# The second gate's row made on chip, and the last four chunks' second weights multiplied by it on GpSimd

## The chip, the cores and the metric

The kernel runs on one core of a Trainium2 chip. The metric is device time in microseconds (us) of one execution; the lower the better. Engines are named as in the profile: PE is TensorE (matmuls; PEld is its weight load), DVE is VectorE, ACT is ScalarE, POOL is GpSimd, and SP is the queue that issues most DMAs.

## The reference

One transformer block on 2048 tokens of width 640 (32 heads of 20), with six modulation rows from a condition vector `c`, and a squared-relu feed-forward layer of width 1728:

```python
mod = (_silu(c) @ w_mod).reshape(c.shape[0], 6, 1, -1)
sa, ca, ga, sb, cb, gb = (mod[:, 0], mod[:, 1], mod[:, 2], mod[:, 3], mod[:, 4], mod[:, 5])
h = _layernorm(x, axis=-1) * (1 + ca) + sa
x = x + ga * _A_ref(h, A_wqkv, A_w_phi, A_wo)
h = _layernorm(x, axis=-1) * (1 + cb) + sb
x = x + gb * _B_ref(h, B_w1, B_b1, B_w2, B_b2)
```

`_A_ref` is linear attention whose feature map is a pair of softmaxes over each head's 20 numbers (`exp` of q and of -q after a small matrix per head); `_B_ref` is `relu(h @ w1 + b1)**2 @ w2 + b2`. The change concerns `gb`, the row of 640 numbers that multiplies the feed-forward result.

## The kernel before

Every fp32 product is made of three fp32r matmuls: each operand is split into a high part (ACT copies it, `AF.Copy`) and a low part (DVE subtracts the high part from the whole, `lo`, line 88), and the terms are high by high, high by low, low by high (`three`, line 78 issues all of them). So each operand of PE costs ACT one copy and DVE one subtraction ahead of it, and the third matmul of a group is the first to need the low part.

Work goes in three stages. First q, k and v are projected for 16 token tiles of 128, and k's and v's sums over tokens are collected. Then, from about 255 us to 389 us, attention's second half runs over eight pairs of tiles, `j` from 0 to 7 in the loop around line 1135: DVE scales the feature rows (`e_prod`, `e_recip`, `e_scale`), PE turns them (`tr_e`, tiles te, whose PSUM banks come from a pool of three), ACT copies them out (tiles ept), PE multiplies by k's and v's sums (`num`), ACT and DVE split that (`num_hi`, `num_lo`, tiles ot), and PE multiplies by the output weights (`do_wo`, tiles pwo). The pair's PE work is interleaved by hand: pair j's four `do_wo` pieces with pair j+1's `tr_e` and `num`. Four q tiles had been put off, and their feature maps are made inside this loop: `q_chain(KEPT + ..., False)` is DVE's part (two reductions, two subtractions, tiles mxq and eq), `exps` is ACT's.

The third stage is the feed-forward layer, eight blocks of 256 tokens (`j` from 0 to 7 again), 14 chunks of 128 hidden columns each (the last has 64), two chunks to a pair `n`. `up` makes a chunk (15 matmuls), ACT applies the relu (line 1250), DVE squares it (line 1251), ACT and DVE split it (`split_a`, tiles ra), and the products with w2 follow one pair later (`down`), between the two `up`s of the next pair. From block 2 on most pairs use seven products in place of eight: DVE makes four sums of quarter tiles (line 1265), ACT and DVE split these (`split_s`, tiles rs), and some combinations of w2's quarters come from DRAM through rings of four SBUF buffers, whose DMAs POOL issues (`t_fetch`, line 1360) when PE has finished with a buffer. The last block takes pairs 4 to 6 plainly. Its accumulators lie in PSUM banks acc (regions 1, 2, 4, 5), acc3x (regions 3 and x share one) and acc67.

The order on PE, DVE, ACT and POOL is written by hand in both later stages (in the third, SP's too, but for block 1); each engine works its queue in order. The gate's row `gb_b` (128 equal rows of 640) multiplies the result of each block (`by_gate`), and `bb` is b2 times that row, added to the residual (`add_bias`, `XR`). In the before kernel the gate lies as a column per 128 numbers (`gate_b`, 128x5); `spread_row` writes it to DRAM number by number and reads it back as a row to all partitions. In the last block the gate multiplies the sum of pairs 0 to 3 (`first_combos`, then `by_gate` at line 1418), and the four quarters of the rest one by one at the very end (`last_downs`): product into the same accumulators, `by_gate` into a spare tile `end`, `add`, `store`.

## Time and profile before

| what | value |
| --- | --- |
| median of 3 runs | 769.13 us (768.96 to 769.65) |
| the profiled execution, its own time | 769.86 us |
| span of its instructions | 768.2 us |
| granted TensorE clock over the span | 1.0 |
| busy share: PE, DVE, ACT, POOL | 99%, 77%, 57%, 19% |

The profiled execution's time is 1.66 us above its span (what lies around the first and last instruction) and 0.73 us above the median. A row of the timeline is: start in us, duration in us, engine, line, operation, output<-inputs, shapes, count; in brackets stands how long the engine sat idle before it and what released it. Consecutive like instructions are merged into one row. A row of the groups ends with busy us and the mean ns of one instruction.

### The profile page before, as it was taken

The page shows a single profiled execution, that of the slowest core. Times are in us where ns is not written, and L with a number is a line of the kernel's source. Part 1 is how long each engine was busy: PE and PEld are TensorE (multiplying, and loading weights), DVE is VectorE, ACT ScalarE, POOL GpSimd, SP SyncE. Part 2 cuts the span into 40 slices and gives each one's busy share as a digit, 9 for nine tenths or more (in the row PEclk, how much of TensorE's full clock was granted, in tenths as well). Part 3 has the DMA queues.
Part 4 walks back from the last instruction along what each step waited for, and adds up shares of the span by engine and source line. Part 5 has one row for each costly group of instructions (what it writes and reads, how often), then busy time and mean ns, then how long its engine had stood idle before and what let it go on. Part 6 is the DMA issues. An engine that isn't in the chain of part 4 may idle for free.

```text
span 768.2 us, 15300 instructions
## 1 busy us (share of the span) xinstructions
PE 759.3 (99%) x5967; PEld 739.8 (96%) x5967; DVE 593.8 (77%) x1083; ACT 434.6 (57%) x971; POOL 144.2 (19%) x301
## 2 busy tenths in 40 slices
PE   9999999999999999999999999999999999999997
PEld 8999999999999989888999999999999999999996
DVE  6598897989999999999565667866767666675666
ACT  5766756767843454545776647465553636445331
POOL 3001101101100255442101000231321313222110
PEclk9999999999999999999999999999999999999999
DMA  9811431343333344155356367996766758766450
GB/s 327 305 65 73 137 103 54 104 139 114 119 104 109 117 142 170 70 80 160 107 180 222 110 226 253 286 323 195 226 181 197 232 177 262 221 184 192 130 165 35
DMA packets 52151, 126.69 MB, mean 165 GB/s; under 512 B 7335, under 2 KB 8103, under 8 KB 52079
## 3 DMA queue, kind: packets, MB, share of 16 engines
q1 hardware_dynamic: 34744, 84.65, 33.1%
q0 software_dynamic: 14752, 35.76, 16.7%
q10 hardware_dynamic: 2583, 5.30, 1.8%
q8 instruction: 47, 0.77, 0.4%
q14 instruction: 25, 0.20, 0.1%
HBM read 95.70 MB, written 29.89 MB: 163 GB/s over the span
## 4 chain that ended last, share of the span: by engine, by line
PE 85%; DVE 8%; issue 2%; DMA 2%; POOL 2%; ACT 1%; SPq 0%; POOLq 0%; DVEq 0%
PE up L78 23%; PE acc L78 17%; PE pk L78 9%; PE pv L78 9%; PE pq L78 8%; PE pwo L78 5%; PE acc3x L78 5%; PE kvp L450 3%; DVE dn L879 2%; DVE scr L877 2%; DVE ezb L901 1%; PE tb L357 1%; PE te L921 1%; DMA ring_b<-td_b 1%; PE ta L357 1%
## 5 line engine op out<-in xcount | busy, mean ns | idle before, releaser
L78 PE MATMUL up<-h,w 128*128 128x256 f32 x1640 | 206.4, 278 | 0.0
L78 PEld LDWEIGHTS up<-h,w 128*128 128x128 f32 x1640 | 196.1, 188 | 0.0
L1250 ACT ACTIVATE ft<-up,b_t 128x256 f32<-128x256 f32 x104 | 48.9, 470 | 115.1 <-PE up L78 114.6
L78 PE MATMUL acc<-w,ra 128*128 128x384 f32 x452 | 97.4, 335 | 0.0
L1251 DVE TENSOR_TENSOR ft<-ft 128x256 f32<-128x256 f32 x104 | 44.1, 424 | 51.2 <-ACT ft L1250 49.6
L78 PE MATMUL pwo<-wo,ot 128*128 128x256 f32 (+3 forms) x512 | 80.8, 312 | 0.6 <-DVE ot L88 0.6
L78 PEld LDWEIGHTS pwo<-wo,ot 128*128 128x128 f32 (+1 forms) x512 | 74.5, 188 | 3.8 <-issue 2.7
L78 PE MATMUL pq<-wq,hT 128*128 128x384 f32 (+1 forms) x480 | 75.2, 312 | 0.0
L78 PEld LDWEIGHTS acc<-w,ra 128*128 128x128 f32 x452 | 72.7, 188 | 0.7 <-DVE ra L88 0.5
L78 PE MATMUL pk<-wk,hT 128*128 128x384 f32 (+1 forms) x480 | 72.7, 308 | 0.0
L78 PE MATMUL pv<-wv,hT 128*128 128x384 f32 (+1 forms) x480 | 71.7, 307 | 0.0
L78 PEld LDWEIGHTS pq<-wq,hT 128*128 128x128 f32 x480 | 71.1, 188 | 0.6 <-issue 0.2
L78 PEld LDWEIGHTS pk<-wk,hT 128*128 128x128 f32 x480 | 70.5, 188 | 0.4 <-issue 0.2
L78 PEld LDWEIGHTS pv<-wv,hT 128*128 128x128 f32 x480 | 70.1, 188 | 0.0
L88 DVE TENSOR_TENSOR ra<-ft,ra 128x384 fp32r<-128x384 f32 (+2 forms) x86 | 36.8, 448 | 32.9 <-ACT ra L1274 20.2
L78 PE MATMUL acc3x<-w,ra 128*128 128x256 f32 x248 | 42.3, 278 | 1.4 <-DVE end L1418 1.4
L1360 POOL DMA_DIRECT2D ring_a<-td_a x34 | 18.3, 537 | 125.5 <-PE acc L78 103.2
L1274 ACT ACTIVATE ra<-ft 128x384 fp32r<-128x384 f32 x48 | 25.2, 526 | 28.4 <-DVE ft L1251 22.4
L78 PEld LDWEIGHTS acc3x<-w,ra 128*128 128x128 f32 x248 | 39.5, 188 | 1.8 <-DVE end L1418 1.6
L1265 DVE TENSOR_TENSOR ft<-ft 128x128 f32<-128x128 f32 x136 | 33.3, 286 | 1.2
L441 DVE TENSOR_REDUCE sk<-ek 128x64 f32<-128x1280 f32 x16 | 23.7, 1484 | 12.4 <-ACT ek L436 10.8
L885 POOL TENSOR_TENSOR dn<-dn,rs_q 128x32 f32<-128x32 f32 x32 | 20.1, 629 | 68.1 <-DVE dn L879 67.8
(264 smaller groups left out, 1406.5 us busy)
## 6 DMA issues: line engine op xcount, KB each, us to landing
ring_c<-td_c POOLq DMA_DIRECT2D x34, 384.0 KB, 4.0
ring_a<-td_a POOLq DMA_DIRECT2D x34, 384.0 KB, 4.1
ring_b<-td_b POOLq DMA_DIRECT2D x34, 256.0 KB, 4.0
esp<-eq SPq DMA_DIRECT2D x12, 640.0 KB, 3.2
el<-esp SPq DMA_DIRECT2D x12, 640.0 KB, 4.0
rw<-in_w SPq DMA_DIRECT2D x23, 320.0 KB, 3.1
wm<-in_w_mod SPq DMA_DIRECT2D x20, 320.0 KB, 3.7
xb<-in_x SPq DMA_DIRECT2D x8, 640.0 KB, 4.0
```

The source lines that it names most:

```text
L78: nc.tensor.matmul(o, a, b, start=first and i == 0, stop=last and i == len(terms) - 1, skip_group_check=skip,)
L88: (eng or nc.vector).tensor_tensor(out_lo, full, hi.bitcast(F32), op=ALU.subtract)
L357: nc.tensor.transpose(p[:, i * P : (i + 1) * P], xn[:, i, d * P : (d + 1) * P], ident)
L441: nc.vector.tensor_reduce(s, heads(flat(e)), axis=AX.X, op=ALU.add)
L450: nc.tensor.matmul(kvp[g // 4][64 * c : 64 * c + 64, a : a + 2 * n].rearrange("p (s n) -> p s n", s=2), v[:, u], e[:, :, o : o + n], start ...
L877: nc.vector.tensor_tensor(z, flat(ET[t]), flat(zb), op=ALU.mult)
L885: nc.gpsimd.tensor_tensor(dn[:, s], dn[:, s], rs[:, 1 - s], op=ALU.mult)
L1250: nc.scalar.activation(r, p, AF.Relu, bias=b1_t[:, f : f + 1])
L1251: nc.vector.tensor_tensor(r, r, r, op=ALU.mult)
L1265: nc.vector.tensor_tensor(t[:, o], t[:, a], t[:, b], op=op)
L1274: nc.scalar.activation(a[:, 0, :3], t[:, :3], AF.Copy)
L1360: nc.gpsimd.dma_start(RING[j, n, r], TD[n][r].bitcast(F32R))
```

## The change

It has three parts.

1. **The gate's row.** `mod_sum(5, gate_b)`, a DVE reduction, moves from the end of pair j = 3 to j = 6. The column is turned by one small PE transpose at j = 7 into 5 rows of 128, copied by ACT (`gate_r`), written to DRAM as whole rows and read back by the same broadcast. b2 is loaded into `bb` itself, early; the product `bb * gb_b` moves from j = 5 to block 0, pair 4.
2. **Attention's orders.** For j = 1 to 5 the second batch of `tr_e` goes (3, 4, 5) in place of (5, 3, 4). At j = 1 DVE's part of the put-off feature map, `q_chain`, stands ahead of `num_lo` in place of behind it.
3. **The end.** The second weights of chunks 10 to 13 are loaded once more in the last block (SP), multiplied by the gate's row on POOL (`gated_mul`, in pairs 1 to 4), and split by ACT and DVE (`gated_split`). So the products of pairs 5 and 6 need no gate: they go to fresh accumulators (`last2`, `last4`, `last3`, `lastx`), in the order 2, 4, 3, x, and at the end one DVE `add` for each follows. The old accumulators are closed after pair 4 and taken through the gate while `up` of pair 6 runs (`piece`). The two bias adds of the last block's residual move from DVE to POOL.

DVE's queue in attention's pair j = 1, before (ezb: scaled features; ot: low parts of the numerator that PE multiplies by the output weights; mxq, eq: the put-off feature map; scr: the next tile's product):

```order
L906 TENSOR_TENSOR ezb_3165<-el_3429,dn_3597 128x80
L88 TENSOR_TENSOR ot_3726<-numa_3727,ot_3726 128x2x256
L88 TENSOR_TENSOR ot_3726<-numb_3728,ot_3726 128x2x256
L88 TENSOR_TENSOR ot_3726<-numc_3729,ot_3726 128x256
L88 TENSOR_TENSOR ot_2_3742<-numc_3729,ot_2_3742 40x256
L430 TENSOR_REDUCE mxq_3769<-eq_2839 128x32
L431 TENSOR_REDUCE mxq_3769<-eq_2839 128x32
L433 TENSOR_TENSOR eq_2839<-eq_2839,mxq_3769 128x640 x2
L877 TENSOR_TENSOR scr_3167<-el_3611,zb 128x1280
```

and the same place after:

```order
L905 TENSOR_TENSOR ezb_3165<-el_3429,dn_3597 128x80
L430 TENSOR_REDUCE mxq_3706<-eq_2840 128x32
L431 TENSOR_REDUCE mxq_3706<-eq_2840 128x32
L433 TENSOR_TENSOR eq_2840<-eq_2840,mxq_3706 128x640 x2
L88 TENSOR_TENSOR ot_3731<-numa_3732,ot_3731 128x2x256
L88 TENSOR_TENSOR ot_3731<-numb_3733,ot_3731 128x2x256
L88 TENSOR_TENSOR ot_3731<-numc_3734,ot_3731 128x256
L88 TENSOR_TENSOR ot_2_3747<-numc_3734,ot_2_3747 40x256
L876 TENSOR_TENSOR scr_3167<-el_3611,zb 128x1280
```

The four instructions of the feature map passed the four that make ot; nothing else moved there.

POOL's queue in the last block's pairs 1 and 2, before (ring: the ring buffers that POOL's DMAs fill; the first number is the pair):

```order
L1360 DMA ring_1_a<-td_a 128x768
L1360 DMA ring_1_b<-td_b 128x512
L1360 DMA ring_2_c<-td_c 128x768
L1360 DMA ring_2_a<-td_a 128x768
L1360 DMA ring_2_b<-td_b 128x512
```

and after, on to the end (w2g: w2's rows as loaded, multiplied in place; xr: the residual):

```order
L1368 TENSOR_TENSOR w2g_8969<-w2g_8969,gb_b 128x640
L1380 DMA ring_1_b<-td_b 128x512
L1380 DMA ring_2_c<-td_c 128x768
L1380 DMA ring_2_a<-td_a 128x768
L1368 TENSOR_TENSOR w2g_9045<-w2g_9045,gb_b 128x640
L1380 DMA ring_2_b<-td_b 128x512
L1380 DMA ring_3_c<-td_c 128x768
L1380 DMA ring_3_a<-td_a 128x768
L1368 TENSOR_TENSOR w2g_9128<-w2g_9128,gb_b 128x640
L1380 DMA ring_3_b<-td_b 128x512
L1368 TENSOR_TENSOR w2g_9207<-w2g_9207,gb_b 128x640
L1667 TENSOR_TENSOR xr_7_0_9210<-xr_7_0_9210,bb 128x640
```

A multiply now stands between the ring DMAs a and b of each pair; the last multiply and the two adds (the second is the queue's last) stand in a row.

DVE's last instructions, before (ft: the chunk; ra: its parts; end: the scratch for the gate; y: the result):

```order
L88 TENSOR_TENSOR ra_6_9396<-ft_6_9393,ra_6_9396 128x128 x2
L1255 TENSOR_TENSOR ft_6_9393<-up_9401,ft_6_9393 64x256
L1256 SCALAR_TENSOR_TENSOR ft_6_9393<-ft_6_9393 64x256
L88 TENSOR_TENSOR ra_6_9396<-ft_6_9393,ra_6_9396 64x256
L1415 TENSOR_TENSOR y_0_9302<-y_0_9302,xr_7_0_9192 128x640
L1415 TENSOR_TENSOR y_1_9303<-y_1_9303,xr_7_1_9194 128x640
L1418 TENSOR_TENSOR end<-acc3x_9076,gb_b 128x256
L1415 TENSOR_TENSOR y_0_9302<-y_0_9302,end 128x256
L1418 TENSOR_TENSOR end<-acc3x_9076,gb_b 128x256
L1415 TENSOR_TENSOR y_1_9303<-y_1_9303,end 128x256
L1418 TENSOR_TENSOR end<-acc_7_9025,gb_b 128x384
L1415 TENSOR_TENSOR y_0_9302<-y_0_9302,end 128x384
```

(region 4's two follow) and after (xr is now the scratch for the gated pieces; last, lastx: the fresh accumulators):

```order
L88 TENSOR_TENSOR ra_6_9422<-ft_6_9419,ra_6_9422 128x128 x2
L1444 TENSOR_TENSOR xr_7_0_9210<-acc_7_9032,gb_b 128x384
L1441 TENSOR_TENSOR y_0_9322<-y_0_9322,xr_7_0_9210 128x384
L1260 TENSOR_TENSOR ft_6_9419<-up_9429,ft_6_9419 64x256
L1261 SCALAR_TENSOR_TENSOR ft_6_9419<-ft_6_9419 64x256
L88 TENSOR_TENSOR ra_6_9422<-ft_6_9419,ra_6_9422 64x256
L1444 TENSOR_TENSOR xr_7_1_9212<-acc_7_9036,gb_b 128x384
L1441 TENSOR_TENSOR y_1_9323<-y_1_9323,xr_7_1_9212 128x384
L1441 TENSOR_TENSOR y_0_9322<-y_0_9322,last_9461 128x384
L1441 TENSOR_TENSOR y_1_9323<-y_1_9323,last_9468 128x384
L1441 TENSOR_TENSOR y_0_9322<-y_0_9322,last_9447 128x256
L1441 TENSOR_TENSOR y_1_9323<-y_1_9323,lastx 128x256
```

Region 2's gated piece (two instructions) now stands between the split of chunk 12 and that of chunk 13, the pieces of regions 3 and x ahead of the rows shown; the final adds have no gate ahead of them.

The diff, cut to its core:

```diff
-        b2s.append(row("s1", "b2s"))
-        nc.sync.dma_start(b2s[0], bass.AP(tensor=b2.tensor, offset=b2.offset, ap=[[0, P], [1, D]]))
+        nc.sync.dma_start(bb, bass.AP(tensor=b2.tensor, offset=b2.offset, ap=[[0, P], [1, D]]))
...
+        if j == 6:
+            mod_sum(5, gate_b)
         if j == 5:
             q_chain(KEPT + 3, False)
             add_x(0, 0, 1)
-            nc.vector.tensor_tensor(bb, b2s[0], gb_b, op=ALU.mult)
...
-            for i, gs in enumerate((range(3), (5, 3, 4))):
+            for i, gs in enumerate((range(3), (3, 4, 5) if te_at[0] == 0 else (5, 3, 4))):
...
+        if j == 1:
+            q_chain(KEPT + SPREAD[j], False)
         do_wo(j, 1, 0)
...
             t2(0, 4)
+            p = tp("gbt")[:NC, :P]
+            nc.tensor.transpose(p, gate_b, ident)
+            nc.scalar.activation(gate_r, p, AF.Copy)
+            nc.sync.dma_start(GD[1], gate_r)
+            nc.sync.dma_start(gb_b, GD[1].rearrange("c p -> (c p)")[None, :].to_broadcast([P, D]))
...
-        if j == 3:
-            mod_sum(5, gate_b)
-            spread_row(1, gate_b, gb_b)
...
+    def gated_mul(f):
+        w = TR_["gated", f]
+        nc.gpsimd.tensor_tensor(w, w, gb_b, op=ALU.mult)
+
+    def gated_split(f):
+        n, t, w = FS[f], W2[f], TR_["gated", f]
+        nc.scalar.activation(t[:, 0], w, AF.Copy)
+        lo(t[:n, 1], w[:n], t[:n, 0])
...
+    def piece(j, r):
+
+        i, c = QUARTERS[r]
+        t = XR[j, i][:, c]
+        by_gate(t, acc(j, r)[1], c)
+        add(Y[j][i][:, c], Y[j][i][:, c], t)
...
+        for r in "3x24":
+            part(NP - 2, r)
+        for r in "243x":
+            part(NP - 1, r)
+            i, c = QUARTERS[r]
+            add(Y[j][i][:, c], Y[j][i][:, c], acc(NB, r)[1])
             store(j, i, c.start, c.stop)
...
+                piece(j, "3")
+                piece(j, "x")
+                up(j, 2 * n)
+                split_a(j, n, (0,))
+                piece(j, "2")
+                up(j, 2 * n + 1)
+                split_a(j, n, (1,))
+                piece(j, "4")
...
+            if (j, n) == (0, 4):
+                nc.vector.tensor_tensor(bb, bb, gb_b, op=ALU.mult)
...
+                if 1 <= n <= 4:
+                    gated_mul(NF - 5 + n)
+                if n == 5:
+                    gated_split(NF - 1)
+                    for i in range(2):
+                        add(Y[j][i], Y[j][i], XR[j, i])
...
             if j == NB - 1 and n == NP - LAST:
+                for i in range(2):
+                    nc.gpsimd.tensor_tensor(XR[j, i], XR[j, i], bb, op=ALU.add)
                 first_combos(j)
+                for i in range(2):
+                    by_gate(Y[j][i], Y[j][i], slice(0, D))
+            if j == NB - 1 and 1 <= n <= 3:
+                gated_split(NF - 5 + n)
```

More of the change, by code (lines that the diff above doesn't have):

```diff
@@ L505 @@
     ga_b = row("s4", "ga_b")
-    b2s = []
     def biases():
-        b2s.append(row("s1", "b2s"))
-        nc.sync.dma_start(b2s[0], bass.AP(tensor=b2.tensor, offset=b2.offset, ap=[[0, P], [1, D]]))
+        nc.sync.dma_start(bb, bass.AP(tensor=b2.tensor, offset=b2.offset, ap=[[0, P], [1, D]]))
     GB = []
@@ L535 @@
     gate_b = const.tile([P, NC], F32, name="gate_b")
+    gate_r = pc.tile([NC, P], F32, name="gate_r")
     LAST_COL = {7: (2, gate_a), 9: (3, cols_b[:, 0:5]), 11: (4, cols_b[:, 5:10])}
@@ L1196 @@
         if j in SPREAD:
-            q_chain(KEPT + SPREAD[j], False)
+            if j > 1:
+                q_chain(KEPT + SPREAD[j], False)
             exps(EQ[KEPT + SPREAD[j]])
-        if j == 3:
-            mod_sum(5, gate_b)
-            spread_row(1, gate_b, gb_b)
         load_e(c + 2)
@@ L1353, in plain_split, with gated_load @@
         lo(t[:, 1], w, t[:, 0])
+    def gated_load(f):
+        n = FS[f]
+        t = TR_["gated", f] = row("s1", f"w2g_{f}")
+        for r in range(P // n):
+            nc.sync.dma_start(t[r * n : r * n + n], w2[f * P : f * P + n])
+    def gated_mul(f):
[5 more added lines that the diff above has]
+        lo(t[:n, 1], w[:n], t[:n, 0])
     def t_fetch(count=1):
@@ L1365, in acc @@
     def acc(j, reg):
+        if j == NB:
+            if (j, reg) not in ACC:
+                ACC[j, reg] = (psC.tile([P, 512], F32, tag="p67" if reg == "3" else "p3x", name=f"last{reg}") if reg in "3x"
+                               else psA.tile([P, 512], F32, tag="pj", name=f"last{reg}", bufs=4))
+            return (j, reg), ACC[j, reg][:, : 256 if reg in "3x" else 384]
         bank_ = {"3": "3x", "x": "3x", "6": "67", "7": "67"}.get(reg, reg)
@@ L1384, in down_plain @@
         regs = (("2", 0, L), ("3", 0, R), ("4", 1, L), ("x", 1, R))
+        last = NF - 1 if j < NB - 1 else NF - 5
         for k in range(2):
@@ L1387, in down_plain @@
             for reg, i, c in regs[2:] if part else regs[:2]:
-                prod(j, reg, block(j, n, (A11, A12, A21, A22)[2 * i + k]), W2[f], c, f == NF - 1, FS[f])
+                prod(j, reg, block(j, n, (A11, A12, A21, A22)[2 * i + k]), W2[f], c, f == last, FS[f])
     def down_pair(j, n, part):
@@ L1446, in finish, with part @@
         store(j, i)
+    QUARTERS = {"3": (0, R), "x": (1, R), "2": (0, L), "4": (1, L)}
+    def piece(j, r):
[3 more added lines that the diff above has]
+        add(Y[j][i][:, c], Y[j][i][:, c], t)
     def last_downs(j):
-        u = p3.tile([P, 8, P], F32, tag="ft", name="end", bufs=2).rearrange("p a b -> p (a b)")
-        at = 0
-        def part(n, r, i, c):
+        def part(n, r):
+            i, c = QUARTERS[r]
             for k in range(2):
                 f = 2 * n + k
-                prod(j, r, block(j, n, (A11, A12, A21, A22)[2 * i + k]), W2[f], c, f == NF - 1, FS[f])
-        def out_(r, i, c, t):
-            by_gate(t, acc(j, r)[1], c)
-            add(Y[j][i][:, c], Y[j][i][:, c], t)
-            store(j, i, c.start, c.stop)
-        regs = ("3", 0, R), ("x", 1, R), ("2", 0, L), ("4", 1, L)
-        for r in regs[:3]:
-            part(NP - 2, *r)
-        for r in regs:
-            if r[0] == "4":
-                part(NP - 2, *r)
-                at = 0
-            part(NP - 1, *r)
-            m = r[2].stop - r[2].start
-            out_(*r, u[:, at : at + m])
-            at += m
+                prod(NB, r, block(j, n, (A11, A12, A21, A22)[2 * i + k]), W2[f], c, f == NF - 1, FS[f])
+        for r in "3x24":
+            part(NP - 2, r)
+        for r in "243x":
+            part(NP - 1, r)
+            i, c = QUARTERS[r]
+            add(Y[j][i][:, c], Y[j][i][:, c], acc(NB, r)[1])
+            store(j, i, c.start, c.stop)
     def prep(n):
@@ L1541 @@
             if (j, n) == (NB - 1, NP - 1):
-                for k in range(2):
-                    up(j, 2 * n + k)
-                    split_a(j, n, (k,))
-                for i in range(2):
-                    add(Y[j][i], Y[j][i], XR[j, i])
+                piece(j, "3")
[6 more added lines that the diff above has]
+                piece(j, "4")
                 break
@@ L1561 @@
             if j >= PLAIN:
-                if n == 5 + (j == PLAIN):
+                if n == 5 + (j == PLAIN) and j < NB - 1:
                     for i in range(2):
@@ L1585 @@
                 gate(j - 1, 1)
+            if j == NB - 1:
+                if n == 0:
+                    plain_load(NP - LAST)
+                    gated_load(NF - 4)
+                if 1 <= n <= 3:
+                    gated_load(NF - 4 + n)
             if n == (5, 5, 5, 3)[min(j, 3)]:
@@ L1590 @@
                     add_bias(j, i)
-            if j == NB - 1 and n == 1:
-                for k in range(NP - LAST, NP - 1):
-                    plain_load(k)
-            if j == NB - 1 and n == 3:
-                for k in range(NP - LAST, NP - 1):
-                    plain_split(k)
-            if j == NB - 1 and n == NP - 2:
-                for i in range(2):
-                    by_gate(Y[j][i], Y[j][i], slice(0, D))
+            if j == NB - 1:
+                if n == 1:
+                    plain_split(NP - LAST)
+                if 1 <= n <= 4:
[4 more added lines that the diff above has]
+                        add(Y[j][i], Y[j][i], XR[j, i])
             up(j, 2 * n + 1)
```

## The prediction

> **What bounds the kernel now.** I read the page's busy shares first, then the waits of PE, then the timeline of attention's second half and of the last block, where the change works.

> ```profile
> PE 759.3 (99%) x5967; PEld 739.8 (96%) x5967; DVE 593.8 (77%) x1083; ACT 434.6 (57%) x971; POOL 144.2 (19%) x301
> PE acc3x L78 <- DVE end L1418: 1.4, 1, 1.4
> ```

> PE is busy for 759.3 of 768.2 us and its matmuls run at the granted clock of 1.0 throughout, so the time changes only where PE waits, where its last product ends, and in what follows that product. PE's longest wait, 1.4 us at the end, is one the change can reach; two more in attention stand in brackets below. The other side matters as much: each wait that the change puts on PE is added in full. Rows between the ones I quote are left out.

> **Attention's orders.** These rows are of pair j = 1 (first seven), then of j = 3 and 4.

> ```profile
> 301.40 4.89 PE L78 MATMUL pwo<-wo,ot 128*128 128x256 f32 x32
> 301.78 0.68 DVE L88 TENSOR_TENSOR ot<-numa,ot 128x512 fp32r<-128x512 f32 x1
> 303.64 0.80 DVE L430 TENSOR_REDUCE mxq<-eq 128x32 f32<-128x640 f32 x1
> 305.19 1.69 DVE L433 TENSOR_TENSOR eq<-eq,mxq 128x640 f32<-128x640 f32 x2
> 306.91 0.74 ACT L436 ACTIVATE eq<-eq 128x640 f32<-128x640 f32 x1 [2.99 <-DVE eq L433]
> 309.18 1.56 ACT L923 ACTIVATE ept<-te 120x512 f32<-120x512 f32 x3
> 309.82 1.63 PE L921 MATMUL te<-ident,ezb 128*80 128x128 f32 x10 [0.33 <-ACT ept L923]
> ...
> 331.19 0.69 DVE L88 TENSOR_TENSOR ot<-numa,ot 128x512 fp32r<-128x512 f32 x1 [0.42 <-ACT ot L950]
> 336.37 0.81 DVE L310 TENSOR_REDUCE gate_b<-mt 128x5 f32<-128x640 f32 x1
> 348.82 0.68 DVE L88 TENSOR_TENSOR ot<-numa,ot 128x512 fp32r<-128x512 f32 x1
> 349.55 2.71 PE L78 MATMUL pwo<-wo,ot 128*128 128x384 f32 x14 [0.57 <-DVE ot L88]
> ```

> The 32 matmuls from 301.40 are the last piece of pair 1 (16) and the first of pair 2; the latter starts at about 303.3, and its third matmul, at about 303.65, is the first to read ot's low part. Before, that part is ready at 301.78 + 0.68 = 302.46. After, the put-off feature map stands ahead of it. DVE is not idle before 301.78 (no bracket), so nothing lets it start sooner; the feature map takes from 303.64 to 305.19 + 1.69 = 306.88, less the overlap of back-to-back starts 3.16 us (the next instruction starts at 306.80). So ot's low part starts at 304.94 and is ready at 305.62: **PE waits 2.0 us** where it waited for nothing.

> What this buys: ACT's exponentials stood idle 2.99 us for the feature map and pushed the copies of te from where PE needed them to 309.18; PE stopped for a bank before 309.82, 0.33 us in the row and about 0.7 with the slower start of the rows around it. With the feature map 1.86 us sooner and PE 2.0 us later, this wait is gone. The wait of 0.57 us before 349.55 (about 0.75 in PE's pace) is for ot's low part of pair 5, which DVE starts at 348.82. DVE there loses the 0.81 us of the gate's reduction (336.37, moved to pair 6), but it was released at 331.19 by ACT's copy of PE's product, so what is left of PE's lateness there (2.0 - 0.7 - 0.1, say 1.2) passes on to it: 348.82 + 1.2 - 0.8 = 349.2, against a PE that comes 1.2 later. This wait goes too. Sum: +2.0 - 0.7 - 0.1 - 0.75 = **+0.45 us**. Bounds: +2.0 if no old wait goes, -1.5 if the new one doesn't come.

> The order (3, 4, 5) of te costs and saves nothing that I can find: the same ten transposes and three copies, and the product that reads them starts 2 us behind them in these rows. The gate's reduction at j = 6, the transpose, ACT's copy of 5 rows and bb's product in block 0 are one instruction each; PE's one transpose is about 0.1 us. The new load of b2 and the row's two DMAs sit on SP's queue ahead of loads that PE doesn't wait for today; I take **+0.1** for all of this, up to 0.5 if a load comes late.

> **The last block: POOL's multiplies.** Before, POOL does nothing here but ring DMAs. Pair 1's rows:

> ```profile
> 723.75 0.53 POOL L1360 DMA_DIRECT2D ring_a<-td_a  x1 [8.99 <-PE acc L78]
> 723.83 0.82 DVE L1418 TENSOR_TENSOR y<-y,gb_b 128x640 f32<-128x640 f32 x1
> 724.68 0.82 DVE L1415 TENSOR_TENSOR y<-y,xr 128x640 f32<-128x640 f32 x1
> 725.60 0.42 DVE L1251 TENSOR_TENSOR ft<-ft 128x256 f32<-128x256 f32 x1
> 726.05 0.52 ACT L1274 ACTIVATE ra<-ft 128x384 fp32r<-128x384 f32 x1 [0.49 <-DVE ft L1251]
> 726.61 0.56 DVE L88 TENSOR_TENSOR ra<-ft,ra 128x384 fp32r<-128x384 f32 x1 [0.59 <-PE acc L78]
> 728.13 1.20 PE L78 MATMUL acc<-w,ra 128*128 128x384 f32 x6
> ```

> The chain for PE is square (725.60), ACT's high part (726.05), DVE's low part (726.61, done 727.17), needed at the third matmul from 728.13, that is 728.48. The slack is 1.3 us. A 128x640 multiply on POOL shows nowhere in this trace; these rows bound it, and show what it does to DVE:

> ```profile
> L198 POOL TENSOR_TENSOR mask<-mask,mtmp 120x60 f32<-120x60 f32 x1 | 0.3, 310 | 0.1
> L203 POOL TENSOR_TENSOR mask<-mask,mtmp 80x40 f32<-80x40 f32 x1 | 0.3, 264 | 0.1
> 289.41 1.49 DVE L901 TENSOR_TENSOR ezb<-el,dn 128x1200 f32<-128x1200 f32 x1
> 289.71 1.30 POOL L886 TENSOR_TENSOR dd<-dd,dn 128x32 f32<-128x32 f32 x1
> 290.82 0.29 DVE L906 TENSOR_TENSOR ezb<-el,dn 128x80 f32<-128x80 f32 x1
> 277.28 0.23 DVE L906 TENSOR_TENSOR ezb<-el,dn 128x80 f32<-128x80 f32 x1
> 196.62 1.98 POOL L345 TENSOR_TENSOR nba<-sma,sqa 128x2 f32<-128x2 f32 x1
> L88 DVE TENSOR_TENSOR w<-rawt,w x4: 807/814/826, 369.2 to 381.1; 128x640 fp32r<-128x640 f32 x4
> ```

> 310 ns for 60 columns and 264 for 40 make 2.3 ns a column and 172 ns fixed, so I estimate 1.64 us for 640 columns, 1.47 of it in the columns. The second thing is exclusion: POOL's addition of 32 columns at 289.71, 0.25 us by that line, lasted 1.30, until DVE's product of two SBUF inputs (289.41 to 290.90) was done; DVE's next such product, dispatched at 290.82, took 0.29 in place of 0.23. So POOL got in at the boundary between two DVE instructions queued back to back, and DVE then waited for it. (The one at 196.62, on two columns, outlasted three DVE products; it is the exception.) I take it that a long POOL multiply does the same: it enters at the next boundary and holds DVE's two-input instructions for 1.47 us. No row shows DVE held that long; the bounds are 0 (it lets DVE through) and 1.64. [...]

> Now pair by pair, with S for what PE has lost so far. Pair 1: the multiply stands behind the ring DMA that ends at 724.28, enters at the gap before 724.68, holds until 726.15. DVE's add then ends at 726.9, the low part of w_8 (0.35) at 727.3, the square at 727.7; ACT's high part 728.2, DVE's low part 728.85, needed 728.48. S = 0.4. Pair 2 begins so late that the multiply enters behind the low part of rs (731.5 to 733.0), ahead of a gate product; square 734.15, low part of ra 735.3, just in time. The rows for pairs 3 and 4 (the first is DVE's four sums, the same in each pair; the second its low part of rs):

> ```profile
> 727.09 1.01 DVE L1265 TENSOR_TENSOR ft<-ft 128x128 f32<-128x128 f32 x4
> 735.91 0.69 DVE L88 TENSOR_TENSOR rs<-ft,rs 128x512 fp32r<-128x512 f32 x1
> 736.75 0.53 POOL L1360 DMA_DIRECT2D ring_a<-td_a  x1 [2.72 <-PE acc L78]
> 737.89 0.68 PE L78 MATMUL acc<-ring_a,rs 128*128 128x384 f32 x3
> 744.39 0.68 PE L78 MATMUL acc<-ring_a,rs 128*128 128x384 f32 x3
> ```

> In front of pair 3's rs DVE now has four sums, a residual add, the 0.81 us low part of w_11 and a square; behind w_11, at 737.85, POOL (ring DMA done at 737.28 + 0.4) enters until 739.3. The square ends 739.7, rs's low part 740.35; PE's third matmul on it stood at 737.89 + 0.35 + 0.4 = 738.65. PE waits 1.75: S = 2.15. From 741.9 POOL has three long instructions in a row (the last multiply and the two adds, their loads landed by then), and DVE gets one instruction between each. DVE's way to rs of pair 3's sums is four sums (1.0), w_12's low part, square, low part of rs, 2.9 us in all; with 3 x 1.47 from 741.93 that ends at 749.2. PE wants it at 744.39 + 0.35 + 2.15 = 746.9. PE waits 2.35: **S = 4.5**. After that POOL is empty. If DVE instead keeps the port while its instructions follow each other, and POOL enters only where DVE waits for ACT, the same walk gives 1.0 to 1.2; with no exclusion it is 0.

> **The end.**

> ```profile
> 753.52 0.76 DVE L88 TENSOR_TENSOR ra<-ft,ra 128x384 fp32r<-128x384 f32 x2 [1.29 <-ACT ra L1274]
> 755.60 1.52 PE L78 MATMUL acc3x<-w,ra 128*128 128x256 f32 x12
> 757.13 0.42 DVE L1256 SCALAR_TENSOR_TENSOR ft<-ft 64x256 f32<-64x256 f32 x1
> 760.43 0.84 PE L78 MATMUL acc3x<-w,ra 128*128 128x256 f32 x5 [1.43 <-DVE end L1418]
> 761.10 2.93 PE L78 MATMUL acc<-w,ra 128*128 128x384 f32 x16
> 764.66 0.56 DVE L1415 TENSOR_TENSOR y<-y,end 128x384 f32<-128x384 f32 x1
> ```

> (Times without S.) PE's wait of 1.43 before 760.43 was for the shared bank of regions 3 and x, 1.6 us with PE's slower start; fresh banks remove it. PE's end, 764.03, would be 762.4. What is late next is chunk 13's part: DVE's low part of ra_5 ends at 754.28 today and about 754.5 with w_13's low part ahead (the 1.29 idle takes most of it). Then come four pieces of 256 columns at 0.42, the square 0.42, ACT's and DVE's split of chunk 12 (about 0.9), region 2's two pieces at 0.56, two instructions at 0.42 (as 757.13), and one of the same columns each on ACT and DVE: 760.5. PE reaches it after 12 short and 15 long matmuls from 755.60, at 755.60 + 1.4 + 15 x 0.18 = 759.7, and waits 0.8; region 4's bank, freed by region 2's piece, costs 0.15. PE ends at 763.3. DVE, with region 4's pieces and four adds behind that, ends at about 763.9, against 764.66 + 0.56 = 765.22. The store behind it is the same wait of about 3 us to 768.2. **-1.3 us**; bounds -2.5 (no new wait) and 0.

> **Sum.** +0.45 + 0.1 + 4.5 - 1.3 = +3.75. The profiled execution's 769.86 (1.66 more than its span) becomes 773.6; it lay 0.73 above the median of 769.13, and the forecast is for the median: **772.9 us**. Differences under 0.2% (1.5 us) count as no change, since a measurement of this kernel tells no less.

> **Rivals.** First, POOL and DVE do not exclude each other for long instructions: S = 0, and the sum is -0.75, 768.4, no change. For it: no row shows DVE held for over 0.1 us. Against it: the row at 289.71, and the 0.06 us by which DVE's own was stretched. 0.17. Second, exclusion holds but DVE keeps the port while its queue is back to back, S = 1.1: +0.35, 769.5. For it speaks the row at 196.62; against it the one at 289.71. The point is whether a waiting POOL instruction or DVE's next one gets the port. 0.15. Third, faster: the new wait at 303.65 doesn't come, because PE's third matmul is not the first to need the low part or DVE is ahead there, and S is 0: -1.55 + 0.1 - 1.3 = -2.75, 766.4. It decides if DVE reaches the feature map 2 us before 301.78. The rows without idle time speak against it. 0.14. Fourth, worse than forecast: 1.64 us holds and late loads, +5.5 or more, 774.6. 0.06. The forecast itself has 0.48, and its own range is 771.5 to 774.2.

> **How the numbers follow.** Faster is the third rival and the lower tail of the first: 0.18. No change is the rest of the first and the second: 0.27. Slower is the forecast, the fourth, and an S of 2 to 3 between the cases: 0.55. Eight in ten from 767.2 to 774.2.

> **What would show it.** Right: a wait of about 2 us of PE on DVE's ot in pair 1 and none at pairs 2 and 5; POOL multiplies of about 1.6 us, longer where they begin under a DVE instruction; DVE two-input instructions of 128x256 that last 1 to 2 us in place of 0.42; PE waits on rs in the last block's pairs 3 and 4 (of 1.75 and 2.35 us); at the end, PE waiting 0.8 us for ra, and the four adds directly behind it. Wrong: DVE's durations in the last block unchanged while POOL multiplies (the first rival), or POOL's multiplies stretched over several DVE instructions and no wait on rs (the second), or no wait for ot before the third matmul of pair 2.

## The result, and the profile after

| | before | after |
| --- | --- | --- |
| median, runs of both on one chip | 769.22 us (768.87 to 770.03, 9 runs) | 774.45 us (771.45 to 778.5, 9 runs) |
| profiled execution, its own time | 769.86 us | 773.49 us |
| span | 768.2 us | 771.4 us |
| granted clock of the runs | 1.0 in the profiled one | 1.0 in two, 0.996 to 0.998 in seven |

The ratio is 1.0064, 95% interval 1.0052 to 1.0077: slower, by about 5 us. The runs of after lie six times as far apart as those of before, and most of them have a clock a little under 1. The profiled execution is one of the two at 1.0.

The waits of PE in after (us in total, times, the longest), where before had 1.4 us on `end`:

```profile
PE pwo L78 <- DVE ot L88: 1.9, 1, 1.9
PE foldk L280 <- DMA raw_k<-in_wk: 1.1, 1, 1.1
...
PE last L78 <- DVE ra L88: 0.8, 1, 0.8
PE up L78 <- ACT ft L1255: 0.7, 1, 0.7
PE acc L78 <- DVE rs L88: 0.6, 1, 0.6
PE acc L78 <- DMA ring_b<-td_b: 0.6, 1, 0.6
```

The first row is the wait at pair 2's third product, the third the one at the end; both had been forecast, at 2.0 and 0.8 us. The fourth and fifth are in the last block. Pair 1 and 2 of attention, PE and DVE:

```profile
306.09 2.71 PE L78 MATMUL pwo<-wo,ot 128*128 128x384 f32 x14 [1.90 <-DVE ot L88]
308.63 1.48 PE L920 MATMUL te<-ident,ezb 128*120 128x128 f32 x12
```

```profile
303.75 1.69 DVE L433 TENSOR_TENSOR eq<-eq,mxq 128x640 f32<-128x640 f32 x2
305.35 0.68 DVE L88 TENSOR_TENSOR ot<-numa,ot 128x512 fp32r<-128x512 f32 x1
...
349.59 0.68 DVE L88 TENSOR_TENSOR ot<-numa,ot 128x512 fp32r<-128x512 f32 x1
```

The feature map stands ahead of ot and PE waits for it; the transposes te behind it run through. The last block, POOL and then DVE:

```profile
725.94 1.77 POOL L1368 TENSOR_TENSOR w2g<-w2g,gb_b 128x640 f32<-128x640 f32 x1
...
736.25 1.56 POOL L1368 TENSOR_TENSOR w2g<-w2g,gb_b 128x640 f32<-128x640 f32 x1 [3.56 <-DVE ft L1270]
...
739.42 1.59 POOL L1368 TENSOR_TENSOR w2g<-w2g,gb_b 128x640 f32<-128x640 f32 x1
...
746.69 1.68 POOL L1368 TENSOR_TENSOR w2g<-w2g,gb_b 128x640 f32<-128x640 f32 x1 [3.29 <-DMA w2g<-in_w]
748.34 3.26 POOL L1667 TENSOR_TENSOR xr<-xr,bb 128x640 f32<-128x640 f32 x2
```

```profile
726.33 2.07 DVE L1441 TENSOR_TENSOR y<-y,xr 128x640 f32<-128x640 f32 x1
...
730.14 1.02 DVE L1270 TENSOR_TENSOR ft<-ft 128x128 f32<-128x128 f32 x4
...
735.57 2.39 DVE L1270 TENSOR_TENSOR ft<-ft 128x128 f32<-128x128 f32 x4
737.88 0.81 DVE L1441 TENSOR_TENSOR y<-y,xr 128x640 f32<-128x640 f32 x1
...
739.36 1.95 DVE L1256 TENSOR_TENSOR ft<-ft 128x256 f32<-128x256 f32 x1
...
748.95 1.22 DVE L1256 TENSOR_TENSOR ft<-ft 128x256 f32<-128x256 f32 x1 [1.99 <-ACT ft L1255]
```

Beside each of the first three multiplies one DVE instruction is long: the residual add 2.07 us in place of 0.81, the four sums 2.39 in place of 1.02, the square 1.95 in place of 0.42. The fourth multiply finds DVE waiting; the square of 1.22 us at 748.95 stands beside the two additions. Two multiplies come late: the second begins at 736.25, right after its load (issued at 728.82) has landed at 736.09, though its row names DVE, and the fourth waited 3.29 us for its load. SP's queue shows why:

```profile
714.30 0.33 SPq L1364 DMA_DIRECT2D w2g<-in_w  x1
728.43 0.34 SPq L1438 DMA_DIRECT2D out<-y  x1
728.82 0.97 SPq L1364 DMA_DIRECT2D w2g<-in_w  x2
738.72 0.34 SPq L1438 DMA_DIRECT2D out<-y  x1
739.16 1.17 SPq L1364 DMA_DIRECT2D w2g<-in_w  x2
```

The loads of chunks 11 to 13 stand behind stores of `out`, and a store waits for DVE: the one at 738.72 waited 8.9 us, by the profile, for the residual add that begins at 737.88 and takes 0.81. The end: one wait of PE, and the last add of DVE right behind PE.

```profile
765.30 2.09 PE L78 MATMUL last<-w,ra 128*128 128x384 f32 x12 [0.78 <-DVE ra L88]
```

```profile
768.00 0.42 DVE L1441 TENSOR_TENSOR y<-y,lastx 128x256 f32<-128x256 f32 x1
```

To place the difference, I matched the matmuls of two profiles in order and took the difference of their start times; a step in it is time lost or gained at that place. Against before, after loses 0.4 at the start (the wait for raw_k, 1.1 in place of 0.5), 0.33 in attention (+2.06 at 306 us, -1.03 at te, -0.54 at 349, the rest in small steps), 0.95 between 380 and 530 us (0.1 of it at the gate's row, the rest in waits for transfers), 2.6 in the last block, and gets back 1.1 at the end.

### The profile page after: what moved, and what is told of

Read it like the earlier page. It is cut to its first block, busy times and chain, and to the rows that moved or that the text cites. A ratio compares the mean times of both kernels' runs of the same rounds, so it can differ in the third digit from the quotient of the medians.

```text
span 771.4 us, 15337 instructions
## 1 busy us (share of the span) xinstructions
PE 760.7 (99%) x5968; PEld 740.4 (96%) x5968; DVE 601.7 (78%) x1088; ACT 437.8 (57%) x975; POOL 154.2 (20%) x307
## 5 line engine op out<-in xcount | busy, mean ns | idle before, releaser
L78 PE MATMUL up<-h,w 128*128 128x256 f32 x1640 | 206.8, 278 | 0.7 <-ACT ft L1255 0.7
L78 PEld LDWEIGHTS up<-h,w 128*128 128x128 f32 x1640 | 196.3, 188 | 1.0 <-ACT ft L1255 1.0
L78 PE MATMUL acc<-w,ra 128*128 128x384 f32 x430 | 93.8, 336 | 0.0
L1256 DVE TENSOR_TENSOR ft<-ft 128x256 f32<-128x256 f32 x104 | 46.3, 446 | 47.5 <-ACT ft L1255 46.1
L78 PE MATMUL pwo<-wo,ot 128*128 128x256 f32 (+3 forms) x512 | 80.8, 312 | 1.9 <-DVE ot L88 1.9
L78 PEld LDWEIGHTS pwo<-wo,ot 128*128 128x128 f32 (+1 forms) x512 | 74.3, 188 | 5.3 <-issue 2.7
L78 PE MATMUL pq<-wq,hT 128*128 128x384 f32 (+1 forms) x480 | 75.2, 312 | 0.0
L78 PE MATMUL pk<-wk,hT 128*128 128x384 f32 (+1 forms) x480 | 72.7, 308 | 0.0
L78 PE MATMUL pv<-wv,hT 128*128 128x384 f32 (+1 forms) x480 | 71.7, 307 | 0.0
L78 PEld LDWEIGHTS pq<-wq,hT 128*128 128x128 f32 x480 | 71.1, 188 | 0.6 <-issue 0.2
L78 PEld LDWEIGHTS pk<-wk,hT 128*128 128x128 f32 x480 | 70.5, 188 | 0.4 <-issue 0.2
L78 PEld LDWEIGHTS acc<-w,ra 128*128 128x128 f32 x430 | 69.0, 188 | 1.3 <-DVE ra L88 1.1
L78 PEld LDWEIGHTS pv<-wv,hT 128*128 128x128 f32 x480 | 70.1, 188 | 0.0
L88 DVE TENSOR_TENSOR ra<-ft,ra 128x384 fp32r<-128x384 f32 (+2 forms) x86 | 37.5, 457 | 32.2 <-ACT ra L1279 21.9
L78 PE MATMUL acc3x<-w,ra 128*128 128x256 f32 x226 | 38.9, 278 | 0.0
L78 PEld LDWEIGHTS acc3x<-w,ra 128*128 128x128 f32 x226 | 36.7, 188 | 0.0
```

The lines of the kernel that those rows point to most:

```text
L78: nc.tensor.matmul(o, a, b, start=first and i == 0, stop=last and i == len(terms) - 1, skip_group_check=skip,)
L88: (eng or nc.vector).tensor_tensor(out_lo, full, hi.bitcast(F32), op=ALU.subtract)
L1256: nc.vector.tensor_tensor(r, r, r, op=ALU.mult)
```

## The experiments

All in one table. "Low clock" counts runs under 0.999; the last four columns are differences to before's profile in us, worked out as above: attention (294 to 380 us), then up to 530 us, the last block (from 727 us on), and the end (the change of the span less what had been lost by then).

| kernel | median us | before beside it | ratio, 95% | low clock | attention | to 530 | last block | end |
| --- | --- | --- | --- | --- | --- | --- | --- | --- |
| after | 774.45 | 769.22 | 1.0064 (1.0052, 1.0077) | 7 of 9 | +0.3 | +0.9 | +2.6 | -1.1 |
| e1 orders only | 770.98 | 769.57 | 1.0026 (1.0015, 1.0037) | 5 of 7 | +1.9 | -0.5 | 0 | -0.1 |
| e2 end only | 771.76 | 769.57 | 1.0032 (1.0021, 1.0044) | 0 of 6 | 0 | +0.3 | +2.3 | -0.9 |
| e3 chain in place | 771.25 | 769.57 | 1.0020 (1.0012, 1.0029) | 0 of 11 | -0.7 | +0.1 | +2.4 | -1.1 |
| e5 no multiplies | 770.81 | 769.57 | 1.0013 (0.9999, 1.0027) | 7 of 9 | +2.0 | -0.1 | 0 | -1.2 |
| e6 transposes in the wait | 775.84 | 769.37 | 1.0087 (1.0073, 1.0101) | 4 of 4 | +4.5 | -0.1 | +2.4 | -1.1 |
| e7 e1 with the chain in place | 768.78 | 769.37 | 0.9997 (0.9988, 1.0006) | 0 of 11 | -0.8 | +1.6 | 0 | 0 |
| e8 e3 without multiplies | 767.75 | 769.37 | 0.9982 (0.9974, 0.9991) | 0 of 11 | -0.7 | -0.4 | +0.3 | -1.8 |
| e9 e3 with early loads | 771.00 | 769.37 | 1.0019 (1.0008, 1.0031) | 2 of 11 | -0.7 | +0.7 | +3.8 | -2.1 |
| e10 e9, multiplies on DVE | 768.13 | 769.33 | 0.9986 (0.9977, 0.9996) | 0 of 11 | -0.7 | +0.3 | +1.0 | -2.0 |
| e11 products in the wait | 772.52 | 769.33 | 1.0047 (1.0034, 1.0060) | 0 of 5 | +0.4 | -0.6 | +3.1 | -1.4 |
| e12 e3, all on DVE, spread | 771.40 | 769.33 | 1.0030 (1.0019, 1.0042) | 0 of 7 | -0.7 | +0.3 | +1.9 | -0.2 |
| e13 e10, additions on DVE | 767.49 | 769.64 | 0.9975 (0.9966, 0.9984) | 0 of 11 | -0.8 | -0.2 | 0 | -2.1 |

The column "to 530" goes from -0.6 to +1.6 without a pattern; in the profiles it is waits for transfers, which differ from one execution to the next. That is why a time in this table is uncertain by more than its profile's own columns.

### The two halves (e1, e2)

e1 takes the diff's lines up to the end of attention and bb's later product; e2 takes all the others.

> Only the first half of the change: attention's orders, the gate's row turned on chip and b2's later multiply; the end is the one of before. Theory one (the terms of the prediction add up, and nothing else is in it): +0.4 in attention and +0.1 for the row, so 769.7 us beside 769.2, with runs as close together as before's (about 1 us) at a granted clock of 1.0. Theory two (the drift of 1.2 us that the trace of after gathers at the start and at waits for transfers, between 0 and 500 us, and the wide spread of its runs belong to this half): 770.5 to 772, runs spread over several us.

> Only the second half: the last four chunks' gated second weights on GpSimd with fresh banks; attention and the gate's row are before's. Theory one (what the trace of after shows of the last block, +2.6 us for VectorE held behind GpSimd and +0.1 to +0.3 of waits on loads, and 1.1 us back at the end): +1.5, so 770.7 us, runs as close as before's. Theory two (the spread of after's runs, 771.5 to 778.5 us, and their granted clock of 0.996 to 0.998 belong to this half): 772 to 774.5 us with a spread of several us. Rival from the prediction (no loss in the last block, only the gain at the end): 768.1 us.

The spread belongs to the orders: e2's runs lie within 1 us at clocks of 0.999 and 1.0, five of e1's seven are at 0.997 or 0.998. So theory two fell for the end. For the orders its number holds (770.98), but by the clock and not by the drift it named: e1's profile has -0.5 us up to 530. e2's median lies 1.1 us above theory one's 770.7, but its profile shows +2.3 and -0.9, as theory one said; the rest of its +2.2 us is 0.3 at the start and 0.3 in waits for transfers. The surprise is in e1's profile. The stretch around the wait, in after (first fence) and in e1; the columns are the window, its length, then busy time and count of PE, PEld, DVE, ACT and POOL, the granted clock, the DMA share and GB/s:

```profile
306.00:307.00 1.00, 0.91 (x5) 0.91 (x6) 1.00 (x4) 1.00 (x3) 0.00 (x0) 1.00 0.30 118
307.00:308.00 1.00, 1.00 (x8) 1.00 (x7) 1.00 (x2) 0.46 (x1) 0.00 (x0) 1.00 0.00 0
308.00:309.00 1.00, 1.00 (x9) 0.95 (x8) 0.97 (x2) 0.17 (x1) 0.00 (x0) 1.00 0.00 0
```

```profile
306.00:307.00 1.00, 1.00 (x6) 1.00 (x7) 1.00 (x3) 1.00 (x3) 0.00 (x0) 1.00 0.10 31
307.00:308.00 1.00, 1.00 (x6) 1.00 (x4) 1.00 (x2) 0.30 (x1) 0.00 (x0) 0.56 0.00 0
308.00:309.00 1.00, 1.00 (x5) 1.00 (x5) 0.97 (x2) 0.00 (x0) 0.00 (x0) 0.50 0.00 0
309.00:310.00 1.00, 1.00 (x5) 0.90 (x4) 1.00 (x2) 0.16 (x1) 0.00 (x0) 0.50 0.00 0
310.00:311.00 1.00, 1.00 (x9) 1.00 (x8) 0.93 (x5) 0.64 (x2) 0.79 (x3) 0.73 0.00 0
```

Behind the wait the granted clock falls to one half. The same fourteen products that took 2.71 us in after's profile take 3.87 here, and the wait ahead of them is the same 1.90 us:

```profile
305.93 3.87 PE L78 MATMUL pwo<-wo,ot 128*128 128x384 f32 x14 [1.90 <-DVE ot L88]
```

By the four lower clocks, 0.44 + 0.50 + 0.50 + 0.27 = 1.7 us of PE's work is lost over about 3.4 us. That is the 1.6 us by which e1's attention stands above after's in the table.

### Attention without the moved chain (e3, e7)

```diff
-        if j == 1:
-            q_chain(KEPT + SPREAD[j], False)
         do_wo(j, 1, 0)
...
         if j in SPREAD:
-            if j > 1:
-                q_chain(KEPT + SPREAD[j], False)
+            q_chain(KEPT + SPREAD[j], False)
             exps(EQ[KEPT + SPREAD[j]])
```

In e3 this is undone in after, in e7 in e1.

> The changed kernel with the query chain of pair 1 put back behind num_lo, where it stood before. Theory one (this move makes the wait of 1.9 us for ot at 306.1 us, and the other orders bring its gains of 1.0 and 0.5 us): the wait goes, PE keeps most of the gains, and the time is 1 to 2 us below the changed kernel's, 772.4 to 773.4 us. Theory two (the move also brings the gain at te, so that both go): 774.0 us, that is 0.4 below at most. Theory three (the wait for ot comes from elsewhere): 774.4 us, and a wait for ot of some 2 us stays in the waits of PE.

> Only the first half of the change, the end as before, and with the query chain of pair 1 where it stood before: the order of the transposes, the earlier sum of the gate, the row turned on chip. Theory one (these orders' gains of 0.3 at te and 0.5 to 0.6 us at 349 us stand without the moved chain, and the row costs 0.1): 0.4 to 0.8 us below before, 768.4 to 768.8 us, clocks as before's. Theory two (the gains hang on the moved chain): 769.2 us. The difference from the half with the moved chain, measured 1.4 us above before, is the price of that move alone with its clock: 1.8 to 2.2 us by theory one.

In e3 the wait for ot is gone, every run is at 0.999 or 1.0, and the median falls 3.2 us (3.5 against the before beside each), more than theory one's 1 to 2. The profiles explain 1.0 of it (attention -0.7 in place of +0.3); the clock, which theory one had left out, gives the rest. Between e7 and e1 the price of that one move is 2.2 us (2.0 against the before beside each), with intervals that don't overlap; e7's 768.78 lies in theory one's range. The other orders keep their gains without it: -0.7 to -0.8 in attention in every kernel with the chain in place. As a time, e7 is not to be told from before.

### Is it the gap that lowers the clock? (e6, e11)

```diff
+        if (t, h) == (4, 0):
+            mm(PWO[t][h][:, :n], terms[:2], last=False)
+            p = tp("fill")
+            for k in range(12):
+                nc.tensor.transpose(p[:, :P], ident, ident)
+            mm(PWO[t][h][:, :n], terms[2:], first=False)
```

> The changed kernel with twelve transposes of the identity matrix (0.11 us each by the rows of te, 1.3 us in all) put into TensorE's wait of 1.9 us for ot at 304 us, behind the second product of pair 2's first half; nobody reads what they write. Theory one (a gap of 1.9 us in a busy TensorE trips the clock gate in most executions: the profiles of two of the last four kernels show a granted clock of 0.50 from 307 to 310 us and half-speed products, 1.5 us in sum, and nothing of the sort where the gap was gone): a gap of 0.6 us is left, every run is at a clock of 0.999 or 1.0, and the median falls from 774.4 to about 772.5 us. Theory two (the lower clock comes from something else in these kernels, such as the load burst at 304 us): clocks of 0.996 to 0.998 stay in most runs, and the median stays at 774.4 us.

This went wrong as a filling. The transposes needed a PSUM tile whose readers were late, and waited themselves; PE stood still for longer:

```profile
306.84 1.50 PE L983 MATMUL fill<-ident 128*128 128x128 f32 x12 [3.24 <-DVE ot L88]
```

All four runs were at 0.997 or 0.998. So it became a test with a longer gap, and it agrees with theory one. e11 fills the gap with products that need nothing new:

```diff
+        if (t, h) == (4, 0):
+            for k in range(4):
+                mm(PWO[t][h][:, :n], terms[:2])
         mm(PWO[t][h][:, :n], terms[a:b], first=(a == 0), last=(b == 16))
```

> The changed kernel with TensorE's wait for ot at 304 us filled by eight more runs of the two products that stand before it (0.173 us each, 1.4 us; they restart the same accumulation, so the output is unchanged and nothing new is waited for): a gap of about 0.5 us stays. The transposes tried before it waited themselves and made the gap 3.2 us, and all four runs fell to 0.997 or 0.998. Theory one (the idle gap trips the clock): every run at 0.999 or 1.0, and the median at 772.3 to 772.8 us, about 2 us below the changed kernel's 774.4. Theory two (the lower clock has another cause in these kernels): clocks of 0.996 to 0.998 in most runs, 774.4 us or a little more.

The gap that is left:

```profile
PE pwo L78 <- DVE ot L88: 0.5, 1, 0.5
```

Five runs of five at 0.999 or 1.0, and 772.5 us, where theory one put it, though ot comes no sooner and PE does 1.4 us of useless work meanwhile. By number of runs, with PE's gap at this place: 3.2 us, 4 of 4 low; 1.9 us (after, e1, e5), 19 of 25 low; 0.5 us, 0 of 5; none (the eight others), 2 of 79, though these have gaps of up to 1.6 us elsewhere, and 1 of the 81 runs of before beside the experiments. The time intervals of e11 and after overlap (e11's ends at 1.0060, after's begins at 1.0052); the clocks don't. It is the idle gap that lowers the clock here; in which executions was not shown, and the last section has an estimate.

### The multiplies (e5, e8)

```diff
     def gated_mul(f):
         w = TR_["gated", f]
-        nc.gpsimd.tensor_tensor(w, w, gb_b, op=ALU.mult)
+        return
```

> The changed kernel without GpSimd's four multiplies: chunks 10 to 13 of the last block stay ungated, so that part of the gate is left out of the output; loads, splits, banks and the two bias additions on GpSimd stay. Theory one (the multiplies hold VectorE's instructions, which makes most of the 2.6 us that PE loses in the last block): 2 to 2.6 us below the changed kernel's, so 771.8 to 772.4 us, and no instruction of VectorE stretched beyond its usual 0.42 or 0.82 us between 720 and 748 us. Theory two (the loss comes from the order of the end, the late loads or the banks): 774 us as before it. Theory three (the multiplies also bring the lower granted clock and the spread): 770 us or below, runs within 1 us of each other.

> The changed kernel with pair 1's query chain in place and without GpSimd's four multiplies (chunks 10 to 13 of the last block are left ungated). Theory one (the multiplies are the loss of the last block, of which the profile of the kernel with the chain in place shows 2.3 us between 728 and 747 us): 2.0 to 2.5 us below that kernel's 771.25, so 768.8 to 769.3 us. Theory two (the end without its gate products gains its 1.1 to 1.3 us in full and the orders 0.4): 767.6 us. Theory three (the late loads and the bank order cost it): 770.5 us or more.

e5 is after with this edit, e8 is e3 with it. In e5 the last block loses nothing, and DVE's rows have their usual lengths, but for one square of 1.29 us at 746.68 beside POOL's two additions; the low clock stays in seven runs of nine, so the multiplies don't bring it. The median, 770.81, is 1 us below theory one's range: from profile to profile 1.0 less is lost up to 530 us and 0.6 less at the start, which theory one had not counted and which the multiplies don't reach. In e8 3.5 us go against e3, theory two's number: 2.1 of loss in the last block, 0.7 that the end then gains more, and 0.5 in waits for transfers. Loads, splits and fresh banks cost next to nothing. Theory three fell in both.

### Early loads (e9)

```diff
-                    gated_load(NF - 4)
-                if 1 <= n <= 3:
-                    gated_load(NF - 4 + n)
+                    for f in range(NF - 4, NF):
+                        gated_load(f)
```

> The changed kernel with pair 1's query chain in place and all four loads of the gated chunks issued at the start of the last block, so that no multiply waits for its load. Theory one, the forecast's (the multiplies fell short of its 4.5 us because the later ones came late, behind their loads, where VectorE had time): in their scheduled places they hold VectorE for all of it, and the time rises by 1 to 2 us, to 772.2 to 773.2 us. Theory two (the late loads cost TensorE, by way of ScalarE that waits behind the late split with the up-product's output): about 0.8 us falls away, 770.4 us. In both, no multiply of GpSimd shows a wait for a load of w2g.

POOL, then DVE, in e9:

```profile
741.54 1.58 POOL L1365 TENSOR_TENSOR w2g<-w2g,gb_b 128x640 f32<-128x640 f32 x1
743.07 3.08 POOL L1663 TENSOR_TENSOR xr<-xr,bb 128x640 f32<-128x640 f32 x2
```

```profile
737.80 2.21 DVE L88 TENSOR_TENSOR rs<-ft,rs 128x512 fp32r<-128x512 f32 x1
...
741.41 5.63 DVE L1267 TENSOR_TENSOR ft<-ft 128x128 f32<-128x128 f32 x4
```

With its loads in time the last multiply and the two additions hold DVE's four sums for 5.63 us in place of 1.02, and PE's loss in the block grows from 2.4 to 3.8 us. That is the forecast's mechanism at nearly its size. But the time stayed (771.0 and 771.25): the end, with the additions out of the way sooner, gains 2.1 in place of 1.1. Neither theory's total held.

### The same products on VectorE (e10, e12, e13)

e10 is e9 with `nc.vector.tensor_tensor` in `gated_mul`.

> The kernel with pair 1's query chain in place and early loads, 771.0 us, and its four multiplies given to VectorE at the same places; the two bias additions stay on GpSimd. Theory one (the loss is the hold: each multiply of 1.57 to 1.77 us on GpSimd keeps a VectorE instruction waiting for about 1.4 us, where VectorE itself needs 0.82 for the product): the last block's loss of 3.7 us falls to some 2 us, and the time to 769.5 to 770.2 us, with no VectorE instruction stretched but by the bias additions. Theory two (VectorE has no room in the last block, so that any work put there moves TensorE by its whole length, and the engine is no matter): 771 us or more.

> The changed kernel with pair 1's query chain in place, all of the gate's products and the bias additions on VectorE, and the products spread: the first one in the block before, where VectorE is busy 2.2 us of 5, the others where it has room in the last block, each load some 6 us ahead of its product. Theory one (what the multiplies cost is a matter of where they stand and of the hold): near the kernel without multiplies, 767.75 us: 767.8 to 768.6 us, below before by 0.1 to 0.2%. Theory two (the last block has no room on VectorE for 2.5 us of products): 769.3 us or more.

e10 is better than either theory's number, and faster than before, by 0.14%; that is less than the 0.2% which the prediction took for a change. What it still loses is the additions on POOL (first fence) on DVE's rows (second):

```profile
739.86 1.71 POOL L1663 TENSOR_TENSOR xr<-xr,bb 128x640 f32<-128x640 f32 x1 [0.59 <-DMA xr<-x]
742.14 1.56 POOL L1663 TENSOR_TENSOR xr<-xr,bb 128x640 f32<-128x640 f32 x1 [0.58 <-DMA xr<-x]
```

```profile
739.85 2.39 DVE L1267 TENSOR_TENSOR ft<-ft 128x128 f32<-128x128 f32 x4
742.16 2.22 DVE L88 TENSOR_TENSOR w<-w2g,w 128x640 fp32r<-128x640 f32 x1
```

e12 (chunk 10's product in block 6, the others in pairs 3 to 5, chunk 12's and 13's loads in pair 3, both additions on DVE at the end of pair 4) missed theory one's range. In the last block up to 752 us nothing is lost, and 0.2 at 714 us, behind chunk 10's product in block 6; then 1.6 us of additions, 1.6 of gate products and chunk 13's product come together on DVE, and ACT and PE wait:

```profile
754.35 3.10 PE L78 MATMUL up<-h,w 128*128 128x256 f32 x25 [1.63 <-ACT ft L1252]
```

Its end gains only 0.2. The number is theory two's, but e10 shows that the last block has room for the products on DVE. So the place counts as much as the engine. e13 is e10 with the two additions on DVE, one each behind the third and fourth multiply, and the residual's loads one pair earlier:

```diff
-            if n == (5, 5, 5, 3)[min(j, 3)]:
+            if n == (5, 5, 5, 3, 3, 3, 3, 2)[j]:
                 residual(j)
...
                     gated_mul(NF - 5 + n)
+                if 3 <= n <= 4:
+                    add_bias(j, n - 3)
```

> The kernel with the four multiplies on VectorE, 768.13 us, whose profile still shows GpSimd's two bias additions (1.71 and 1.56 us) stretching VectorE's four products from 1.02 to 2.39 us and one subtraction from 0.82 to 2.22 us, and 0.9 us lost at 745 us. Here the additions stand on VectorE too, one behind the third multiply and one behind the fourth, and the residual rows' loads one step earlier. Theory one (that hold is what is left of the loss): 0.4 to 0.9 us less, 767.2 to 767.7 us, no stretched instruction of VectorE between 720 and 750 us. Theory two (VectorE has nothing left in that stretch, so 1.6 us of additions cost as much there as the hold): 768.1 us or up to 0.8 more.

The waits of PE in e13, from the longest on:

```profile
PE warm L625 <- POOL bdc L155: 1.1, 1, 1.1
PE te L920 <- ACT ept L922: 0.5, 1, 0.5
PE last L78 <- DVE ra L88: 0.3, 1, 0.3
PE acc L78 <- DMA ring_b<-td_b: 0.2, 1, 0.2
```

No wait on rs or up is left, the block loses nothing and the end gains 2.1: 767.49 us, ratio 0.9975 (0.9966 to 0.9984), theory one's range, faster than both kernels. Against e10 alone the two intervals overlap.

## Why the prediction was right, and where it was not

The sign and the mechanism were right, two sizes were off, and one cost was not seen at all. From profile to profile the sum was +3.75 and came out as 773.49 - 769.86 = 3.63. That these agree so closely is luck: the last block's term came out 1.9 short, and 0.4 at the start, 0.8 in waits for transfers, 0.2 less gained at the end and 0.4 outside the span (773.49 lies 2.1 above its span, before's time 1.66) made up for it. The median, 774.45, lies just above 774.2, the upper end of the stated range.

**Attention's orders, +0.45.** Measured +0.33 at a clock of 1.0: the wait 1.90 (2.0 forecast), te's wait gone for 1.0 (0.7), pair 5's 0.54 (0.75; DVE began ot at 349.59, not at 349.2), and -0.16 in small steps, where the sum had a -0.1 that no row of it shows. The step that failed is the pricing of the new wait by its length alone, from "its matmuls run at the granted clock of 1.0 throughout". That was true of before. The gap of 1.90 us lowered it in 19 of 25 executions, and in e1's profile that costs 1.6 us more. This is why the median, 774.45, stands above the forecast of 772.9, while the profile agrees with the sum.

**The gate's row, +0.1.** PE's step there is +0.10. A late load was the bound, 0.5. The wait for raw_k makes 0.4 at the start, but the other kernels with the same loads lie between -0.6 and +0.3 there; the waits for transfers before 530 us came to 0.8 in after's profile, but the column ranges from -0.6 to +1.6 over the other kernels. So I put both to the execution and not to the change.

**The last block, +4.5.** Exclusion held for the long instructions here, as argued from 0.06 us: DVE's square of 0.42 us took 1.95 beside a multiply of 1.59. The multiply's estimate of 1.64 us lies between the shortest and the longest (1.56 and 1.77). The size was wrong: 2.6 us. Pair 1 gave 0.2 (0.4 forecast). Pair 3 gave 1.65 (1.75), in two parts: 0.84 where PE waited for ACT, which stood behind its copy of the late chunk 11, and 0.81 for rs. Pair 4 gave 0.3 (2.35), and PE shows no wait on rs there. The other 0.4 lies in the rows behind the waits, where PE is slower: the 15 products at 739.00 took 1.99 us, where those at 734.91 and 743.28, with no wait ahead of them, took 1.86. The failed step is "their loads landed by then": the forecast did not follow SP's queue, where the stores of out hold the loads back, and so the last multiply began at 746.69, and the additions fell where PE had less to lose. With the loads in time (e9) the same term is 3.8. The rows of pair 3's first part, ACT and then PE:

```profile
737.85 0.74 ACT L1372 ACTIVATE w<-w2g 128x640 fp32r<-128x640 f32 x1 [2.78 <-POOL w2g L1368]
```

```profile
739.00 1.99 PE L78 MATMUL up<-h,w 128*128 128x256 f32 x15 [0.67 <-ACT ft L1255]
```

**The end, -1.3.** Measured -1.1, with PE's wait of 0.78 us for ra (0.8) and the four adds right behind PE. In e8, e9, e10 and e13 the end gains more, 1.8 to 2.1, within the bound of 2.5; why e5, which has no multiplies either, gains only 1.2 was not settled.

**The rivals.** The first (no exclusion) and the second (DVE goes first while its queue is full) fell with the stretched rows: above all with e9's four sums, 5.63 us in place of 1.02 beside POOL's three instructions. The third fell with the wait at 306 us. The fourth gave nearly the right time, 774.6, for another reason: no hold of 1.64 us and no more loss by late loads, but the clock. That is luck, too.

**Still open.** Two of after's runs, 777.59 and 778.5 us at a clock of 0.996, lie 3 us above its others at 0.997 and 0.998, and no profile caught such a run. A clock of 0.996 would be about 0.004 x 771 / 0.5 = 6 us at half speed, an estimate; these need not be two stretches, since e1's mean of 0.997 is already below the 0.998 that its one stretch makes, 1 - 1.7 / 769.8. Nor was it settled what lowered the clock in two of e9's runs and in one of before's own (772.53 us at 0.997), where the gap at 304 us is not there.

## What to carry to other kernels

Price a new wait of a busy TensorE by its length and by what the clock does behind it: look at the granted clock of all runs, not only of the profiled one, when a change opens a gap of about 2 us (here 1.90 us, and 19 of 25 runs low), and close the gap or fill it (with 0.5 us left, none of five was low). An elementwise product on GpSimd was not free work beside a busy VectorE: its 1.6 us held VectorE for 1.3 to 1.5 us at a time, where VectorE itself needed 0.82; given to VectorE, and put where it has room, the same change is a gain. And when a moved step depends on a load, follow the queue that issues the load as closely as the engine that uses it.
